# One-token decode of two attention layers and two gelu layers on one core: two K loads split into thin row groups, and three addresses and cuts moved around one V load

## The chip, the cores and the metric

The kernel runs on one core of one Trainium2 chip. The metric is the device time of one execution in microseconds (us), lower is better. Before the change three runs took 679.94, 680.22 and 680.78 us; the median is 680.22 us.

## The reference

One token (x, 512 numbers) goes through the same pair of layers twice: attention over a cache of 4096 positions with 32 heads of 128, then a gelu layer of 1376. All is float32.

```python
def _A_ref(x, k_cache, v_cache, wq, wo):
    q = (x @ wq).reshape(B, Sq, H, Dh).transpose(0, 2, 1, 3)
    scores = jnp.einsum("bhqd,bhkd->bhqk", q, k_cache) * (Dh ** -0.5)
    p = softmax(scores)
    o = jnp.einsum("bhqk,bhkd->bhqd", p, v_cache)
    return o.transpose(0, 2, 1, 3).reshape(B, Sq, H * Dh) @ wo

def _B_ref(x, w1, b1, w2, b2):
    return jnp.einsum("bsf,fd->bsd", gelu(x @ w1 + b1), w2) + b2

x = x + _A_ref(_layernorm(x), k_cache, v_cache, wq, wo)
x = x + _B_ref(_layernorm(x), w1, b1, w2, b2)
x = x + _A_ref(_layernorm(x), k_cache, v_cache, wq, wo)
x = x + _B_ref(_layernorm(x), w1, b1, w2, b2)
```

K and V are 67 MB each and are needed in both layers. SBUF does not hold them, so nearly all of both is read from HBM twice.

## The kernel before, in words

The 32 heads are worked on in G = 8 groups of J = 4. Each group has a K block and a V block of 128 partitions x 16384 numbers (8.39 MB, 64 KB a partition), and a pair of weights (a wo and a wq, 2.10 MB together). A block is cut into C = 8 chunks of 4 units; a unit (U) is 512 columns, and a chunk NC is 4 units.

All big data lies in one SBUF tile, `arena`, whose places are given by hand: three homes for blocks, A_AT, C_AT and B_AT, each 32 units long, then SHARED, SCRATCH and PAIR. Loads are made by `load` (L68 to L71): one DMA of 128 partitions, issued on SyncE's queue (SP), and kept in the order of the program. SP works through its list strictly in order: where a load must wait (for an earlier DMA, or for TensorE or another engine to be done with the place that it overwrites), every later load waits behind it. Issued transfers run on 16 DMA engines that each take their share in the order of issue.

For each group TensorE (PE) first makes the `scores` of the eight K chunks (L190), 4 matmuls a chunk. Then come the largest score, the exponentials and the sum (DVE and ACT, L195 to L218), and then `values` (L220), the product with the eight V chunks, 4 matmuls a chunk. `head_out` (L225) gathers the result (DVE writes to SCRATCH at L227 and reads it at L231) and multiplies it by wo; `next_queries` (L308) makes the next group's queries from wq. Both multiply with the pair that was loaded to PAIR, or to C_AT at the turn between the layers.

Layer one (L321 to L346) goes through groups 0 to 7; K of group g goes to RING[2g % 3] and V to RING[(2g + 1) % 3]. The generator `blocks` (L288) issues a load a piece and hands out the chunks. The last group's blocks are cut into pieces (HALVES, LAST), so that work can begin before all has landed.

At the turn, group 7's K and V and most of group 6's V are still in SBUF. So layer two goes through the groups from 7 down. Its first group (n = 0) needs no load; its second (n = 1) loads only K, in six pieces, to wherever room is, the last and longest (14 units, L374) to C_AT + 8U to C_AT + 22U. Behind it goes the pair for n = 1 (L375), to C_AT + 22U to C_AT + 30U. Six units of group 6's V were set aside in PSUM (pK) and are copied back by ACT (L384 to L387), two of them to C_AT + 30U and C_AT + 31U, where they are the values of chunk 6, j = 2 and 3. So the home C holds, while n = 1 runs: K up to unit 22, the pair up to unit 30, and two units of V.

From n = 2 on (L397) each group loads K, V and a pair again. K of n = 2 goes to A_AT and V of n = 2 to C_AT, in two pieces, five chunks and three (L403). The first needs the scores of n = 1 to be done with C's first 20 units, and the second needs the pair to be done with, which ends with `next_queries(2)` (L394).

Of the kernel before, what the change touches and what calls it, by code (L numbers as in the profile page):

```python
# [17 lines left out]
P = 128  # L18
# [5 lines left out]
C = 8  # L24
# [4 lines left out]
U = 512  # L29
NC = 4 * U  # L30
# [6 lines left out]
A_AT, B_AT, C_AT = RING  # L37
# [3 lines left out]
PAIR = SHARED + 11 * U  # L41
ARENA = PAIR + 2 * NC
HALVES = ((0, 4), (4, 8))
W1_AT_END = ((0, 2), (2, 3), (3, 4))
LAST = ((0, 4), (4, 6), (6, 7), (7, 8))
# [5 lines left out]
def decode_layers(ctx: ExitStack, tc: tile.TileContext, x, k, v, w, w1, b1, w2, b2, out):  # L51
    nc = tc.nc
# [12 lines left out]
    def at(first, n):  # L65
        return arena[:, first : first + n]

    def load(first, src):  # L68
        t = at(first, src.shape[-1])
        tc.keep_in_program_order(nc.sync.dma_start(t, src))  # L70
        return t  # L71

    def matmul(*a, **kw):
        tc.keep_in_program_order(nc.tensor.matmul(*a, **kw))  # L74

    def quarters(first):
        return [at(first + U * j, U) for j in range(4)]

    def part(src, g, a, b):
        return src[g][:, NC * a : NC * b]  # L80

    def of_w(row, i, n):
        return w[row][:, NC * i : NC * (i + n)]

    def by_four(t):
        return t.rearrange("p (j n) -> p j n", j=4)


    wq_t = by_four(load(SHARED, of_w(1, 0, 1)))
    b1c, b2c = ctile("b1c", FB), ctile("b2c", 4)  # L90
    xcol = ctile("xcol", 4)
# [62 lines left out]
    def idle(to, n=U):  # L154
        matmul(to[:, :n], zero[:, 0:1].to_broadcast([P, P]), at(C_AT, n), start=True, stop=True)
# [34 lines left out]
    def scores(z, c, kt):  # L190
        for j in range(J):
            matmul(pS[32 * j : 32 * j + C, :], z[:, j, C - 1 - c : 2 * C - 1 - c], kt[j],
                   start=(c == 0), stop=(c == C - 1))

    def exponentials(sc, nsc):  # L195
        nc.vector.tensor_reduce(ml[:, 0:1], pS, axis=AX.X, op=ALU.max)  # L196
        mt, m, bias = small("mt", 32), small("m"), small("mt", 32)
        nc.vector.transpose(mt, ml)
        nc.vector.tensor_reduce(m, mt[:, :C], axis=AX.X, op=ALU.max)
        nc.vector.tensor_scalar(mb[:, :C], m.to_broadcast([P, C]), nsc, None, op0=ALU.mult)  # L200
        nc.vector.transpose(bias, mb)  # L201
        p = at(SCRATCH, U)
        nc.scalar.activation(p, pS, AF.Exp, bias=bias[:, 0:1], scale=sc, accum_out=ml[:, 0:1])  # L203
        return p

    def weights(p):
        for b in range(4):
            tc.keep_in_program_order(nc.tensor.transpose(  # L208
                pT[:, b].rearrange("p j r -> p (j r)"), p[:, P * b : P * (b + 1)], ident))
        pt = work.tile([P, P], F32, name="turned").rearrange("p (j c b) -> p j c b", j=J, c=C)  # L210
        nc.vector.tensor_copy(pt, pT[:, :, :, :C].rearrange("p b j c -> p j c b"))  # L211
        lt, l, lr, rl = small("mt", 32), small("l"), small("mt", 32), small("rl")
        nc.vector.transpose(lt, ml)  # L213
        nc.vector.tensor_reduce(l, lt[:, :C], axis=AX.X, op=ALU.add)
        nc.vector.tensor_copy(lb, l.to_broadcast([P, 32]))
        nc.vector.transpose(lr, lb)
        nc.vector.reciprocal(rl, lr[:, 0:1])
        return pt, rl  # L218

    def values(i, pt, vt, c):  # L220
        for j in range(J):
            matmul(pO[32 * j : 32 * j + 4, :], pt[:, j, c, :], vt[j],
                   start=(i == 0), stop=(i == C - 1))

    def head_out(rl, wt, last=False):  # L225
        ot = at(SCRATCH, U)
        nc.vector.transpose(ot, pO)  # L227
        o, on = small("o", 4), on_wide
        own = at(SCRATCH, 4 * 129).rearrange("p (b q) -> p b q", q=129)[:, :, :P]
        own = own.rearrange("p b (d q) -> p d b q", q=32)[:, :, :, 0]  # L230
        nc.vector.tensor_reduce(o, own, axis=AX.X, op=ALU.add)  # L231
        if last:
            nc.vector.tensor_scalar(on[:, :4], o, rl, None, op0=ALU.mult)
        else:
            nc.vector.tensor_scalar(in_quarters(on, 4), o.unsqueeze(1).to_broadcast([P, J, 4]), rl, None,  # L235
                                    op0=ALU.mult)
        for d in range(4):
            if last:
                for j in range(J):
                    matmul(pS[32 * j : 32 * j + 1, :P], on[:, d : d + 1], wt[:, d, P * j : P * (j + 1)],  # L240
                           start=(d == 0), stop=(d == 3))
            else:
                matmul(pO, on[:, d : d + P], wt[:, d, :], start=(d == 0), stop=(d == 3))
        return of_32(turned(pS) if last else turned(pO, wide=True), 4)
# [34 lines left out]
    def load_w1(first, a, b):  # L279
        load(first + W1C * a, w1[:, W1C * a : W1C * b])  # L280

    def load_w2(first, a, b):
        load(first + U * a, w2[:, U * a : U * b])
# [1 line left out]
    def in_rows(first, n, rows):  # L285
        return [at(first + n * i, n) for i in range(rows)]

    def blocks(src, g, home, pieces=((0, C),)):  # L288
        for a, b in pieces:
            load(home + NC * a, part(src, g, a, b))  # L290
            for c in range(a, b):
                yield c, quarters(home + NC * c)

# [14 lines left out]
    def next_queries(n, xs, negm, wt):  # L308
        for c in range(4):
            matmul(pO, xs[:, 2 * c : 2 * c + P], wt[:, c, :], start=(c == 0), stop=(c == 3))  # L310
        return queries(n, negm, wide=True)

    def add_up(acc, own):
        t = small("acc", 4)
        nc.vector.scalar_tensor_tensor(t, own, 1.0, acc, op0=ALU.mult, op1=ALU.add)
        return t
# [4 lines left out]
    for g in range(G):  # L321
        final = g == G - 1
        k_home, v_home = RING[2 * g % 3], RING[(2 * g + 1) % 3]
        for c, t in blocks(k, g, k_home, HALVES if final else ((0, C),)):
            scores(z, c, t)
        pt, rl = weights(exponentials(sc, nsc))
        for c, t in blocks(v, g, v_home, LAST if final else ((0, C),)):
            values(c, pt, t, c)
            if final and c > 4:
                idle(pS)  # L330
            if g == G - 2:
                for j in range(J):
                    i = 4 * c + j - KEPT_V // U
                    if i >= 0:
                        nc.scalar.copy(pK[i], t[j])
        if final:
            wo_t = by_four(load(PAIR, of_w(g % 2, g, 1)))
            for i in range(3):
                load_w1(SHARED, i, i + 1)
            own = head_out(rl, wo_t, last=True)  # L340
            load_w1(SHARED, 3, 4)
        else:
            pair = load(PAIR, of_w(g % 2, g, 2))
            acc = add_up(acc, head_out(rl, by_four(pair[:, :NC])))
            wq_t = by_four(pair[:, NC:])
            z = next_queries(g + 1, xs, negm, wq_t)  # L346
# [8 lines left out]
    g = G - 2  # L355
# [5 lines left out]
    def begin_k(home, n):  # L361
        a = len(k_t)
        load(home, k[g][:, U * a : U * (a + n)])
        k_t.extend(at(home + U * i, U) for i in range(n))
# [4 lines left out]
    for c in range(C):  # L369
# [2 lines left out]
            begin_k(C_AT + NC * c, 4)  # L372
        if c == 5:
            begin_k(C_AT + 2 * NC, 14)  # L374
    pair = load(C_AT + 22 * U, of_w(g % 2, g - 1, 2))  # L375
    p = exponentials(sc, nsc)
    z = next_queries(1, xs, negm, wq_t)
    pt, rl = weights(p)
# [2 lines left out]
    acc = add_up(acc, head_out(rl, wo_t))  # L381

    v_t = [at(B_AT + U * i, U) for i in range(KEPT_V // U)]
    for i, first in enumerate([C_AT + 30 * U, C_AT + 31 * U] + [PAIR + U * j for j in range(4)]):  # L384
        t = at(first, U)
        nc.scalar.copy(t, pK[i])
        v_t.append(t)  # L387
# [9 lines left out]
    for n in range(2, G):  # L397
        g, final = G - 1 - n, n == G - 1
        k_home, v_home = homes[(2 * n - 1) % 3], homes[2 * n % 3]
        for c, t in blocks(k, g, k_home, HALVES if final else ((0, C),)):  # L400
            scores(z, c, t)
        pt, rl = weights(exponentials(sc, nsc))
        for c, t in blocks(v, g, v_home, LAST if final else ((0, 5), (5, 8)) if n == 2 else ((0, C),)):  # L403
            values(c, pt, t, c)
            if final and c > 4:
                idle(pS)
        if final:
            wo_t = by_four(load(PAIR, of_w(g % 2, g, 1)))
            for a, b in W1_AT_END:
                load_w1(A_AT, a, b)  # L410
            for a, b in W2_AT_END:
                load_w2(A_AT + 11 * U, a, b)
            own = head_out(rl, wo_t, last=True)
        else:
            pair = load(PAIR, of_w(g % 2, g - 1, 2))
            acc = add_up(acc, head_out(rl, by_four(pair[:, NC:])))
            z = next_queries(n + 1, xs, negm, by_four(pair[:, :NC]))
# [47 lines left out]
```

## Time and profile before

| | us |
|---|---|
| median of three runs | 680.22 |
| the profiled execution's own time | 679.55 |
| its span, first to last instruction | 677.8 |
| PE busy | 433.1 (64%) |
| weight loads | 119.4 (18%) |
| DVE busy | 110.7 (16%) |
| ACT busy | 22.2 (3%) |
| bytes moved | 286.56 MB, mean 423 GB/s |

The profile shows one execution. Times on a timeline are counted from the span's start. A row of the SP queue gives the start of an issue, what the issue itself took, the line and what is written and read; "x2" merges two issues into one row, whose length then holds the waiting between them. A line of the list of transfers gives the size and the time from the issue to the last byte's landing. A window row gives for a stretch the busy time of each engine, TensorE's granted clock, the share of time in which the DMA engines were busy, and the rate.

### The profile page before, as it was taken

To read this page: it belongs to the slowest core of one execution; us is meant where nothing else is said; L and a number is where in the kernel's file an instruction comes from. 1 tells how busy PE (TensorE), PEld (TensorE's weight loads), DVE (VectorE), ACT (ScalarE), POOL (GpSimd) and SP (SyncE) were. 2 spreads that over 40 slices of the span, in tenths; PEclk is the share of its full clock that TensorE was granted. 3 is DMA by queue.
4 is the path that set the end of the run, shared out by engine and by line. 5 is a ranking of instruction groups with operands and counts; after the bars stand their busy time and mean duration, and the time that the engine had idled before them with its cause. 6 is when DMAs were issued, how large, how long until landed. Compare 5 with 4: busy or idle time off the path is not lost. (4 is left out here: it accounts for less than half of the span.)

```text
span 677.8 us, 6359 instructions
## 1 busy us (share of the span) xinstructions
PE 433.1 (64%) x2792; PEld 119.4 (18%) x2792; DVE 110.7 (16%) x431; ACT 22.2 (3%) x47; POOL 4.3 (1%) x21
## 2 busy tenths in 40 slices
PE   1547666485554874667777897686455764766776
PEld 0112112121111211111113222221111111211112
DVE  1012101111021101210212312211021011210211
ACT  0010000000000000001000110000000000000000
POOL 1000000000000000000000000000000000000000
PEclk9969768797698876977979998998698776977977
DMA  9999999999999999999999999899999999999997
GB/s 372 434 433 433 435 433 433 416 449 437 430 433 413 451 433 430 433 431 422 428 413 359 426 459 414 358 468 441 427 433 398 465 433 423 437 430 410 426 416 294
DMA packets 11404, 286.56 MB, mean 423 GB/s; under 512 B 1776, under 2 KB 1776, under 8 KB 3440
## 3 DMA queue, kind: packets, MB, share of 16 engines
q1 hardware_dynamic: 10944, 286.14, 98.7%
q8 instruction: 22, 0.36, 0.2%
q10 hardware_dynamic: 432, 0.01, 0.0%
q14 instruction: 6, 0.05, 0.0%
HBM read 286.14 MB, written 0.00 MB: 422 GB/s over the span
## 5 line engine op out<-in xcount | busy, mean ns | idle before, releaser
L74 PE MATMUL pO<-arena,turned 128*4 128x512 f32 x1024 | 144.8, 726 | 76.8 <-DMA arena<-in_v 75.6
L74 PE MATMUL pS<-arena,zq 128*8 128x512 f32 x1024 | 137.7, 698 | 70.8 <-DMA arena<-in_k 65.4
L74 PE MATMUL pO<-arena,x_wide 128*128 128x512 f32 (+1 forms) x176 | 54.9, 508 | 24.4 <-DVE turned L137 18.1
L74 PE MATMUL pO<-arena,on_wide 128*128 128x512 f32 x112 | 51.8, 605 | 18.6 <-DVE on_wide L235 18.6
L74 PEld LDWEIGHTS pS<-arena,zq 128*8 128x8 f32 x1024 | 29.1, 99 | 176.3 <-issue 167.1
L74 PEld LDWEIGHTS pO<-arena,turned 128*4 128x4 f32 x1024 | 27.6, 97 | 183.8 <-issue 179.5
L137 DVE STREAM_TRANSPOSE turned<-pO 32x128 f32<-32x128 f32 x112 | 35.0, 312 | 101.1 <-PE pO L74 99.9
L227 DVE STREAM_TRANSPOSE arena<-pO 128x512 f32<-128x512 f32 x16 | 11.5, 717 | 220.4 <-PE pO L74 220.4
L208 PE MATMUL pO<-ident,arena 128*128 128x128 f32 x64 | 14.5, 368 | 43.9 <-ACT arena L203 42.4
L196 DVE TENSOR_REDUCE ml<-pS 128x1 f32<-128x512 f32 x16 | 11.1, 692 | 185.0 <-PE pS L74 185.0
L74 PEld LDWEIGHTS pO<-arena,x_wide 128*128 128x128 f32 (+1 forms) x176 | 21.6, 155 | 57.1 <-DVE turned L137 26.5
L203 ACT ACTIVATE arena<-pS,mt,sc 128x512 f32<-128x512 f32 x16 | 12.4, 777 | 523.7 <-DVE mt L201 523.7
L74 PEld LDWEIGHTS pO<-arena,on_wide 128*128 128x128 f32 x112 | 20.1, 189 | 51.7 <-DVE on_wide L235 31.6
L208 PEld LDWEIGHTS pO<-ident,arena 128*128 128x128 f32 x64 | 9.3, 181 | 58.6 <-ACT arena L203 51.3
L74 PE MATMUL pO<-arena,x 128*2 128x344 f32 x64 | 7.2, 531 | 5.0 <-DMA arena<-in_w 4.4
L74 PE MATMUL pS<-arena,zero 128*128 128x512 f32 x16 | 9.9, 706 | 0.0
L74 PE MATMUL pS<-arena,gelu_g 128*1 128x128 f32 x176 | 6.7, 290 | 1.5 <-DVE gelu_g L270 1.3
L213 DVE STREAM_TRANSPOSE mt<-ml 128x32 f32<-128x32 f32 x16 | 3.4, 212 | 17.2 <-ACT arena L203 17.2
L74 PEld LDWEIGHTS pS<-arena,gelu_g 128*1 128x1 f32 x176 | 3.9, 88 | 7.4 <-DVE gelu_g L270 3.7
L211 DVE COPY turned<-pO 128x128 f32<-128x128 f32 x16 | 4.4, 277 | 3.1 <-PE pO L208 3.1
L74 PE MATMUL pO<-arena,zero 128*128 128x512 f32 x8 | 4.5, 644 | 0.0
L248 POOL TENSOR_TENSOR xb<-x,b2c 128x4 f32<-128x4 f32 x2 | 0.4, 200 | 636.9 <-DVE x L148 636.9
(71 smaller groups left out, 76.5 us busy)
## 6 DMA issues: line engine op xcount, KB each, us to landing
arena<-in_w SPq DMA_DIRECT2D x13, 2048.0 KB, 28.8
arena<-in_k SPq DMA_DIRECT2D x4, 4096.0 KB, 42.5
arena<-in_v SPq DMA_DIRECT2D x2, 4096.0 KB, 47.6
arena<-in_w SPq DMA_DIRECT2D x6, 1024.0 KB, 20.3
arena<-in_v SPq DMA_DIRECT2D x1, 5120.0 KB, 23.8
arena<-in_w SPq DMA_DIRECT2D x6, 688.0 KB, 30.2
arena<-in_v SPq DMA_DIRECT2D x2, 2048.0 KB, 50.8
arena<-in_v SPq DMA_DIRECT2D x4, 1024.0 KB, 53.3
```

The lines of the kernel that those rows point to most:

```text
L74: tc.keep_in_program_order(nc.tensor.matmul(*a, **kw))
L137: nc.vector.transpose(t[q], src[q, P * j : P * (j + 1)])
L196: nc.vector.tensor_reduce(ml[:, 0:1], pS, axis=AX.X, op=ALU.max)
L203: nc.scalar.activation(p, pS, AF.Exp, bias=bias[:, 0:1], scale=sc, accum_out=ml[:, 0:1])
L208: tc.keep_in_program_order(nc.tensor.transpose(pT[:, b].rearrange("p j r -> p (j r)"), p[:, P * b : P * (b + 1)], ident))
L211: nc.vector.tensor_copy(pt, pT[:, :, :, :C].rearrange("p b j c -> p j c b"))
L213: nc.vector.transpose(lt, ml)
L227: nc.vector.transpose(ot, pO)
L248: nc.gpsimd.tensor_tensor(xb, pairs(xs)[:, :, 0], b2c, op=ALU.add)
```

## The change

It has two parts that share no line.

First, a new helper `load_uneven` issues half a K block as nine DMAs: seven of 16 rows, each of every eighth partition, and the remaining 16 rows as two of eight. It is used for the second half of K of group 1 in layer one and of n = 3 in layer two; the first half is one DMA of 128 rows.

Second, at the turn the pair for n = 1 moves up by two units, to C_AT + 24U to C_AT + 32U, and the two units of V move below it, to C_AT + 22U and 23U. V of n = 2 is cut after six chunks and no longer after five.

```diff
+    def load_uneven(first, src):
+
+        t = at(first, src.shape[-1])
+        for rows in (*(slice(k, P, 8) for k in range(7)), slice(7, 64, 8), slice(71, P, 8)):
+            tc.keep_in_program_order(nc.sync.dma_start(t[rows], src[rows]))
...
-    def blocks(src, g, home, pieces=((0, C),)):
+    def blocks(src, g, home, pieces=((0, C),), uneven=False):
         for a, b in pieces:
-            load(home + NC * a, part(src, g, a, b))
+            (load_uneven if uneven and a else load)(home + NC * a, part(src, g, a, b))
...
-        for c, t in blocks(k, g, k_home, HALVES if final else ((0, C),)):
+        for c, t in blocks(k, g, k_home, HALVES if final or g == 1 else ((0, C),), g == 1):
...
-    pair = load(C_AT + 22 * U, of_w(g % 2, g - 1, 2))
+    pair = load(C_AT + 24 * U, of_w(g % 2, g - 1, 2))
...
-    for i, first in enumerate([C_AT + 30 * U, C_AT + 31 * U] + [PAIR + U * j for j in range(4)]):
+    for i, first in enumerate([C_AT + 22 * U, C_AT + 23 * U] + [PAIR + U * j for j in range(4)]):
...
-        for c, t in blocks(k, g, k_home, HALVES if final else ((0, C),)):
+        for c, t in blocks(k, g, k_home, HALVES if final or n == 3 else ((0, C),), n == 3):
...
-        for c, t in blocks(v, g, v_home, LAST if final else ((0, 5), (5, 8)) if n == 2 else ((0, C),)):
+        for c, t in blocks(v, g, v_home, LAST if final else ((0, 6), (6, 8)) if n == 2 else ((0, C),)):
```

Only SP's list gains instructions. The first place is the start of layer one on SP, before the change: K and V of group 0, the first pair, then K and V of group 1. A name in brackets is the counter that the issue waits for: DMAHW0 to DMAHW7 are the eight counters that the DMAs use in turn, PE, DVE and Activation count the work of those engines.

```order
L70 DMA arena<-in_k 128x16384
L70 DMA arena<-in_v 128x16384 [waits DMAHW1_49,PE_49]
L70 DMA arena<-in_w 128x4096
L70 DMA arena<-in_k 128x16384
L70 DMA arena<-in_v 128x16384 [waits DMAHW4_49,DMAHW0_49,PE_49]
L70 DMA arena<-in_w 128x4096 [waits DMAHW6_49,PE_49]
```

The same place after the change, from the first pair on:

```order
L70 DMA arena<-in_w 128x4096
L70 DMA arena<-in_k 128x8192
L77 DMA arena<-in_k 16x8192 [waits DMAHW0_49,DVE_49]
L77 DMA arena<-in_k 16x8192
L77 DMA arena<-in_k 16x8192 [waits DMAHW2_49]
L77 DMA arena<-in_k 16x8192 [waits DMAHW3_49]
L77 DMA arena<-in_k 16x8192 [waits DMAHW4_49]
L77 DMA arena<-in_k 16x8192 [waits DMAHW5_49]
L77 DMA arena<-in_k 16x8192 [waits DMAHW6_49]
L77 DMA arena<-in_k 8x8192 [waits DMAHW7_49]
L77 DMA arena<-in_k 8x8192 [waits DMAHW0_49]
L70 DMA arena<-in_v 128x16384 [waits DMAHW1_49,PE_49]
```

K of group 1 waited for nothing, and V of group 1 for the scores of group 0. Now the first thin transfer waits for DVE: the count is that of the gathering read of group 0 (L231 of before). The first eight-row transfer waits for the landing of the first half (its counter is DMAHW7), the second for the landing of the first thin transfer, and V of group 1 for the landing of the second thin one. The second use, at n = 3, has the same shape, with the gathering read of n = 2.

The second place is SP's list at the turn, from the longest piece of K of n = 1 to K of n = 3. Before:

```order
L70 DMA arena<-in_k 128x7168 [waits PE_49]
L70 DMA arena<-in_w 128x4096 [waits PE_49]
L70 DMA arena<-in_k 128x16384 [waits DMAHW0_49,PE_49]
L70 DMA arena<-in_v 128x10240 [waits DMAHW5_49,DMAHW4_49,DMAHW6_49,DMAHW1_49,PE_49]
L70 DMA arena<-in_v 128x6144 [waits DMAHW2_49,DMAHW7_49,PE_49,Activation_49]
L70 DMA arena<-in_w 128x4096 [waits DMAHW3_49,Activation_49]
```

After:

```order
L70 DMA arena<-in_k 128x7168 [waits PE_49]
L70 DMA arena<-in_w 128x4096 [waits PE_49]
L70 DMA arena<-in_k 128x16384 [waits DMAHW1_49,PE_49]
L70 DMA arena<-in_v 128x12288 [waits DMAHW5_49,DMAHW6_49,DMAHW2_49,DMAHW7_49,PE_49,Activation_49]
L70 DMA arena<-in_v 128x4096 [waits DMAHW3_49,DMAHW0_49,PE_49]
L70 DMA arena<-in_w 128x4096 [waits DMAHW4_49,Activation_49]
```

The order of the loads stays. The first piece of V takes over the wait for the copied units of V (Activation), and its count of PE work moves from the scores of n = 1 to the last matmul of chunk 6 of the values of n = 1, since that matmul reads the unit at C_AT + 23U. The second piece still waits for the last matmul of `next_queries(2)`.

## Prediction

> **What bounds the kernel now.** I read the page first: the span, the busy share of the DMA engines in 40 slices, and what the queues carried.
>
> ```profile
> span 677.8 us, 6359 instructions
> DMA  9999999999999999999999999899999999999997
> GB/s 372 434 433 433 435 433 433 416 449 437 430 433 413 451 433 430 433 431 422 428 413 359 426 459 414 358 468 441 427 433 398 465 433 423 437 430 410 426 416 294
> q1 hardware_dynamic: 10944, 286.14, 98.7%
> q8 instruction: 22, 0.36, 0.2%
> ```
>
> The DMA engines are busy in nearly every slice, and queue q1, which carries the loads, fills 98.7% of their time. At 433 GB/s its 286.14 MB need 661 us of a span of 677.8 us, so only some 17 us are not plain transfer. Then I asked for the long stretches of both layers by windows.
>
> ```profile
> 70.00:340.00 270.00, 169.57 (x955) 45.23 (x956) 41.49 (x151) 9.26 (x20) 0.00 (x0) 0.81 1.00 431
> 440.00:630.00 190.00, 119.94 (x669) 32.31 (x670) 30.04 (x110) 3.56 (x9) 0.00 (x0) 0.81 1.00 433
> ```
>
> The last two columns are the DMA share and the rate: 1.00 at 431 and 433 GB/s. One of the 16 engines thus moves 433 / 16 = 27.1 GB/s. TensorE is busy for under two thirds of either stretch. Last the chain of waits, three of its pieces:
>
> ```profile
> 460.20 47.76 DMA arena<-in_k
> ...
> 547.47 47.70 DMA arena<-in_k
> ...
> 601.64 46.91 DMA arena<-in_v
> ```
>
> Where a layer runs steadily, the chain is made of transfers alone. So three things count here: bytes, pauses of the stream, and how evenly the 16 engines finish, since a block has landed when the last of them has. The bytes do not change. The sum is made against the profiled execution's own 679.55 us, 0.67 us under the median of 680.22.
>
> **The cut of V at the turn.** The slice with 358 GB/s is the turn. SP's timeline, the windows there and the list of transfers:
>
> ```profile
> 381.19 0.33 SPq L70 DMA_DIRECT2D arena<-in_w  x1
> 394.39 0.33 SPq L70 DMA_DIRECT2D arena<-in_k  x1
> 406.36 22.77 SPq L70 DMA_DIRECT2D arena<-in_v  x2
> ...
> 398.00:416.00 18.00, 14.86 (x116) 3.59 (x118) 3.95 (x16) 2.35 (x5) 0.00 (x0) 0.91 1.00 433
> ...
> 428.00:431.00 3.00, 1.36 (x10) 0.23 (x12) 1.48 (x5) 0.00 (x0) 0.00 (x0) 1.00 0.65 164
> ...
> arena<-in_k SPq DMA_DIRECT2D x1, 23.7
> ...
> arena<-in_v SPq DMA_DIRECT2D x1, 5120.0 KB, 23.8
> ...
> arena<-in_v SPq DMA_DIRECT2D x1, 3072.0 KB, 9.8
> ...
> L70 SPq DMA_DIRECT2D arena<-in_v x1: 328/328/328, 428.8 to 428.8; - x1
> ...
> 410.19 8.40 PE L74 MATMUL pO<-arena,turned 128*4 128x512 f32 x64 [0.38 <-DVE turned L211]
> ...
> 441.55 8.09 PE L74 MATMUL pO<-arena,turned 128*4 128x512 f32 x64 [0.38 <-DVE turned L211]
> ```
>
> K of n = 2 lands at 394.4 + 23.7 = 418.1 us, and five chunks of V at 406.4 + 23.8 = 430.2. The other three were issued at 428.8, when `next_queries(2)` was done with the pair, and landed 9.8 us later. Their 3.15 MB take 7.3 us at 433 GB/s, so an issue to an empty stream costs 2.5 us before it flows, and the flow began at 431.3: a pause of 1.1 us after 430.2 for the engine that was last, and of more for the others (164 GB/s from 428 to 431).
>
> After the change the first piece may go only when the values of n = 1 are through chunk 6: the 28th of 32 products, at 410.19 + 28/32 x 8.40 = 417.5 us (the row counts two matmul records a product). With 2.5 us it flows from 420.0. K has landed by 418.1, so the pause is 1.9 us, at a place where the windows show none (1.00, 433 GB/s up to 416). Its six chunks (6.29 MB, 14.5 us) then run until 434.5, and the last two, issued at 428.8 as before, follow without a pause. The pause of 1.1 us goes, one of 1.9 us comes: **+0.8 us**. If the lead-in were 2 us and not 2.5, both would shrink by the same half microsecond; only if K landed 1.9 us later against TensorE would both be hidden, so this term lies between 0 and +1. TensorE meets no V wait from it: the values of n = 2 began at 441.5 us, and 434.5 + 4.8 for the last two chunks is 439.3.
>
> Pair and copies cost nothing: the pair now waits for the last two products of the scores too, under 0.5 us, while the 3.67 MB of K ahead of it (8.5 us) are still in flight. The two units copied by ACT go to a place that is free earlier than the old one. If that cover were gone, the half microsecond would be paid.
>
> **The thin transfers: are they issued in time?** They wait for DVE's gathering read, with everything on SP behind them.
>
> ```profile
> 9.21 0.43 SPq L70 DMA_DIRECT2D arena<-in_k  x1
> 35.11 0.33 SPq L70 DMA_DIRECT2D arena<-in_v  x1
> ...
> arena<-in_k SPq DMA_DIRECT2D x1, 61.0
> ...
> 56.47 0.18 DVE L231 TENSOR_REDUCE o<-arena 128x4 f32<-128x16 f32 x1
> ...
> 450.46 0.18 DVE L231 TENSOR_REDUCE o<-arena 128x4 f32<-128x16 f32 x1
> ...
> arena<-in_k SPq DMA_DIRECT2D x1, 34.7
> ...
> 429.65 0.43 SPq L70 DMA_DIRECT2D arena<-in_k  x1
> 437.46 0.33 SPq L70 DMA_DIRECT2D arena<-in_v  x1
> ```
>
> K of group 1 landed at 9.2 + 61.0 = 70.2 us, its first half (4.19 MB, 9.7 us) thus at 60.5. The read ends at 56.65; with 2.5 us the thin transfers flow from 59.2, 1.3 us early. At n = 3 the half lands at 429.6 + 34.7 - 9.7 = 454.6 and the read ends at 450.64: 1.5 us early. Nine issues at 0.43 us are 3.9 us of SP's time; a 16-row transfer puts one row of 32 KB on each engine, 1.21 us at 27.1 GB/s, so the queue grows. V behind them was issued at 35.11 and at 437.46; now it waits for the second thin transfer's landing, at 60.5 + 2 x 1.21 = 62.9, and has to go by 70.2 - 2.5 = 67.7. All of this is covered, by about 1 us at the tightest; beyond that each microsecond of a late read would be paid. The halved K lets scores begin earlier, which gains nothing: the transfers behind them set the pace.
>
> **The thin transfers: do they flow and balance?** Seven of them give every engine a row. The two of eight rows leave it open which eight engines move them. If one is moved by one half and the other by the other, all engines carry eight rows as before, and the price is 0. If both go to the same eight, these carry nine rows and the others seven: +1.21 and -1.21 us for an engine, in each layer. The trace shows that engines do end apart:
>
> ```profile
> 670.00:672.00 2.00, 1.80 (x22) 0.60 (x24) 0.69 (x4) 0.21 (x1) 0.00 (x0) 0.50 0.96 388
> 672.00:673.00 1.00, 1.00 (x36) 0.73 (x32) 0.00 (x0) 0.00 (x0) 0.00 (x0) 0.81 0.58 234
> 673.00:674.00 1.00, 0.82 (x33) 0.49 (x28) 0.00 (x0) 0.00 (x0) 0.00 (x0) 1.00 0.40 145
> ```
>
> With nothing left behind them, about half of the engines are still at work 1 to 2 us after the first have ended. If the late ones are those relieved, up to 1.21 us a layer is gained; if any late one is among those loaded, 1.21 us is lost, since the last one counts. Which they are the trace does not say. [...] So the price lies between -1.2 and +1.2 us a layer; I take +0.4, on the side of a loss: **+0.8 us** for two. [...]
>
> Sum: +0.8 + 0.8 = +1.6 us, 681.15 for the profiled execution, 681.8 as a median. Own range of this case: from 0, below which lies the balance case of the rivals, to the upper ends, +1 and twice +1.2: 680.2 to 683.6.
>
> **The rivals.** About 0.2%, or 1.4 us, is what a measurement of this kernel can tell from no change.
>
> Thin transfers at half rate. For: no transfer of this trace has fewer than 128 rows or leaves out partitions, so the 27.1 GB/s of an engine are shown only for whole transfers; rows eight partitions apart may meet at the same few ways into SBUF while others lie idle. Against: nothing in this trace. If two engines share what one had, a row takes 2.42 us. Engines with seven rows need 16.9 us, those with nine 21.8, where 9.7 stood: +7.3 to +12.1 us in each of two layers, all on the path since the stream is the bound. With the cut of V that is +15.4 to +25.0, less up to 2 us a layer where the engines that were late are not those loaded; I would say 701. [...] The same mechanism in part (a row at 1.5 us) would give 685 to 688.
>
> Balance works (faster). The late engines of both layers are all in the relieved half: -1.2 us at each layer's end, +0.8 from V: 680.2 - 1.6 = 678.6. For: the ends lie 1 to 2 us apart, about what one row moves between the halves. Against: the engine that ends last has to be one of the relieved, and no engine of the loaded half may be over 1.2 us late, in both layers. It decides from the point where the gain of the two passes the 0.8 us of the turn.
>
> The change does nothing: the two eight-row transfers spread over both halves and the turn's two pauses weigh the same for the stream: 680.2.
>
> **How the numbers follow.** Full rate with small losses 0.43, half rate (or part of it) 0.35, balance works 0.14, nothing 0.08. Faster by over 0.2% (under 678.9): the better part of the balance case and a little of the others, 0.14. Within 0.2%: the case of nothing and the lower part of the likeliest (0 to +1.4 us), 0.24. Slower: the rest of it and the half rate, 0.62. The predicted time is that of the likeliest. The range has to reach to half rate, since 0.35 cannot be left out: from 679.2, which leaves out most of the balance case, to 704.5, which leaves out only its very end. Most of the chance lies at both ends of this range and little between 684 and 695.
>
> **What would show it.** Each thin transfer's landing tells the rate: steps of 1.2 us between successive ones at full rate, 2.4 at half. V of group 1 landing when it did before, or 7 to 12 us later, says the same. At the turn the DMA share should drop below 1 between 416 and 420 us and stay near 1 from 428 to 431 (all counted against the same event of TensorE). Balance shows at the end of the stream: fewer or more engines busy in the last 2 us. The prediction is wrong in its mechanism if the pause at the turn does not move, if the thin transfers start late, or if the stream runs slower than 27.1 GB/s an engine within them.

## The result and the profile after

The changed kernel takes 712.07 us (median of six runs, 709.71 to 714.09), the kernel before 680.50 us beside it (six runs, 679.71 to 682.26). The ratio is 1.0458, with a 95% interval of 1.0443 to 1.0474: 31 us slower, outside the range given. The profiled execution took 710.45 us, its span 708.7.

Four lines of the page of the changed kernel: the span, the busy share of the DMA engines and the rate in 40 slices, and the queue of the loads.

```profile
span 708.7 us, 6399 instructions
...
DMA  9999999999999999999999998999999999999996
GB/s 415 412 414 285 275 417 449 434 419 440 440 419 429 449 414 441 441 409 434 422 404 346 431 454 354 415 293 231 414 456 433 426 436 418 445 430 422 427 415 268
...
q1 hardware_dynamic: 11456, 286.14, 98.4%
```

The bytes are the same and the engines are as busy as before. But two pairs of slices move 285 and 275, 293 and 231 GB/s, where the kernel before moved 433 and 435, 468 and 441, and the busy share there is still 9. Each pair is a place where a half K goes in thin transfers. So the stream does not pause there; it runs slowly. Windows of the changed kernel show it in the first of the two places, with the DMA share and the rate in the last two columns:

```profile
59.00:80.00 21.00, 9.31 (x45) 2.78 (x43) 2.89 (x10) 0.00 (x0) 0.00 (x0) 0.89 1.04 206
62.00:72.00 10.00, 7.29 (x40) 2.21 (x40) 1.97 (x8) 0.00 (x0) 0.00 (x0) 1.00 1.00 211
...
86.00:200.00 114.00, 65.22 (x388) 17.04 (x380) 16.01 (x60) 2.61 (x6) 0.00 (x0) 0.81 1.00 431
```

211 GB/s at a share of 1.00 is 13.2 GB/s an engine. A row of 32 KB takes 2.48 us instead of 1.21. Behind the thin transfers the rate is 431 again, as it was.

What it costs is read where TensorE meets the loads. Its timeline before, at the values of group 1 (layer one) and of n = 3 (layer two):

```profile
89.75 9.89 PE L74 MATMUL pO<-arena,turned 128*4 128x512 f32 x64 [6.18 <-DMA arena<-in_v]
...
483.85 9.12 PE L74 MATMUL pO<-arena,turned 128*4 128x512 f32 x64 [7.40 <-DMA arena<-in_v]
```

And after, with the scores of the second half K ahead of each:

```profile
83.84 6.21 PE L80 MATMUL pS<-arena,zq 128*8 128x512 f32 x32 [12.40 <-DMA arena<-in_k]
103.10 8.55 PE L80 MATMUL pO<-arena,turned 128*4 128x512 f32 x64 [9.20 <-DMA arena<-in_v]
...
495.79 5.04 PE L80 MATMUL pS<-arena,zq 128*8 128x512 f32 x32 [17.23 <-DMA arena<-in_k]
514.74 9.23 PE L80 MATMUL pO<-arena,turned 128*4 128x512 f32 x64 [10.51 <-DMA arena<-in_v]
```

Values of group 1 begin at 103.10 instead of 89.75, 13.4 us later; those of n = 3 at 514.74 instead of 483.85, 30.9 us later. In both the bracket names the load as what ended the wait, so these are landings. Practically the whole loss stands at these two places, and none of it is won back. SP's timeline after:

```profile
57.02 8.37 SPq L77 DMA_DIRECT2D arena<-in_k  x9
67.40 0.34 SPq L70 DMA_DIRECT2D arena<-in_v  x1
```

The nine thin transfers are issued from 57.0 us on, and V behind them at 67.4, long before the thin ones have landed. Issue was not the trouble.

### The profile page after: what moved, and what is told of

Its sections match the earlier page's. It is cut to its first block, busy times and chain, and to the rows that moved or that the text cites. A ratio compares the mean times of both kernels' runs of the same rounds, so it can differ in the third digit from the quotient of the medians.

```text
span 708.7 us, 6399 instructions
## 1 busy us (share of the span) xinstructions
PE 433.9 (61%) x2792; PEld 119.5 (17%) x2792; DVE 110.4 (16%) x431; ACT 22.2 (3%) x47; POOL 4.3 (1%) x21
## 5 line engine op out<-in xcount | busy, mean ns | idle before, releaser
L80 PE MATMUL pO<-arena,turned 128*4 128x512 f32 x1024 | 146.7, 734 | 85.0 <-DMA arena<-in_v 83.7
L80 PEld LDWEIGHTS pO<-arena,on_wide 128*128 128x128 f32 x112 | 20.1, 189 | 51.7 <-DVE on_wide L241 31.6
## 6 DMA issues: line engine op xcount, KB each, us to landing
arena<-in_w SPq DMA_DIRECT2D x6, 688.0 KB, 30.1
```

## The experiments

What had to be told apart: ways into SBUF, as I supposed them, that the rows under way share (theory 1), a fixed time for each transfer that is not overlapped (theory 2), and the reading side, where 16 streams 512 KB apart might collide (theory 3). Then the size of the other terms: the cut of V, and the nine and seven rows. Costs in us are the ratio less 1, times 680.5, with the 95% interval. Rates are taken from the window 62 to 72 us, which lies within the thin transfers; only in the two kernels that flow at nearly the full rate does its end belong to the V behind them. The share of a short window can pass 1, so the rate is divided by it. A transfer of 16 rows is 524 KB. The diffs show the lines that matter, and "..." stands for what is left out.

**The two parts alone.** Only the cut of V, with the pair and the two copied units:

```diff
-    pair = load(C_AT + 22 * U, of_w(g % 2, g - 1, 2))
+    pair = load(C_AT + 24 * U, of_w(g % 2, g - 1, 2))
...
-    for i, first in enumerate([C_AT + 30 * U, C_AT + 31 * U] + [PAIR + U * j for j in range(4)]):
+    for i, first in enumerate([C_AT + 22 * U, C_AT + 23 * U] + [PAIR + U * j for j in range(4)]):
...
-        for c, t in blocks(v, g, v_home, LAST if final else ((0, 5), (5, 8)) if n == 2 else ((0, C),)):
+        for c, t in blocks(v, g, v_home, LAST if final else ((0, 6), (6, 8)) if n == 2 else ((0, C),)):
```

> Only the move of the pair behind chunk six of C and the cut of the third V into six and two chunks; K loads as before. If the thin transfers carry nearly all of the 31.6 us that the change cost, this kernel is slower than before by 0.8 us (my term, 0 to +1) to 1.4 us (what the landings of V behind the turn gained on those of K in the changed kernel: +15.9 against +14.5 us), so 681.3 to 681.9. If the cut had a cost that shows only later (a pair or copy that comes late), it is slower by over 2 us.

Measured 681.42, ratio 1.0013 (1.0001 to 1.0025): +0.9 us (0.1 to 1.7). Windows at the turn, of the kernel before and then of this one; 428 to 431 before was 0.65 and 164 GB/s:

```profile
416.00:420.00 4.00, 2.67 (x29) 0.47 (x17) 1.13 (x3) 0.00 (x0) 0.00 (x0) 1.00 0.88 379
...
412.00:442.00 30.00, 22.53 (x148) 6.49 (x140) 6.65 (x24) 0.87 (x2) 0.00 (x0) 0.96 0.91 382
```

```profile
416.00:420.00 4.00, 2.67 (x25) 0.54 (x18) 1.13 (x3) 0.00 (x0) 0.00 (x0) 1.00 0.66 197
428.00:431.00 3.00, 1.35 (x10) 0.23 (x12) 1.48 (x5) 0.00 (x0) 0.00 (x0) 1.00 1.13 481
...
412.00:442.00 30.00, 22.53 (x148) 6.67 (x144) 6.65 (x24) 0.87 (x2) 0.00 (x0) 0.96 0.89 371
```

The pause has moved from 428 to 431 to 416 to 420. Over the 30 us around both it costs (382 - 371) x 30 us = 0.33 MB, or 0.8 us at 433 GB/s.

Only the thin transfers:

```diff
-        for c, t in blocks(k, g, k_home, HALVES if final else ((0, C),)):
+        for c, t in blocks(k, g, k_home, HALVES if final or g == 1 else ((0, C),), g == 1):
...
-        for c, t in blocks(k, g, k_home, HALVES if final else ((0, C),)):
+        for c, t in blocks(k, g, k_home, HALVES if final or n == 3 else ((0, C),), n == 3):
```

> Only the thin K transfers of both layers; the cut of V as before. If the two edits add up, 31.6 less 0.8 to 1.4: slower than before by 30 to 31 us, 710.5 to 711.5, some 15 us per layer. If the cut of V pushed the second use into a worse place, the thin transfers alone cost less than 28 us.

Measured 706.94, ratio 1.0383 (1.0364 to 1.0403): +26.1 us (24.8 to 27.4), below what was expected. The two parts make 27.0 us, the whole 31.2 (30.1 to 32.3).

**What makes the rows slow?** The same half K in eight transfers of columns, all 128 rows each (this kernel and the others of this part change the same lines and leave the cut of V as before):

```diff
-        for rows in (*(slice(k, P, 8) for k in range(7)), slice(7, 64, 8), slice(71, P, 8)):
-            ...dma_start(t[rows], src[rows])
+        for k in range(8):
+            cut = slice(n * k, n * k + n)
+            ...dma_start(t[:, cut], src[:, cut])
```

> The same two half Ks in eight transfers of 512 KB, each 1,024 columns of all 128 rows, so that one engine still gets eight pieces and the issue count stays about the same. If the half rate comes from which rows are under way together (rows eight apart share only half of the ways into SBUF), these run at the full 27 GB/s per engine: 680.2 to 682 in all, a step of 1.2 us between landings. If it comes from cutting a load into many small transfers (a fixed price for each, some 1.2 us per transfer in the changed kernel's steps of 2.5 us), the cost stays: 8 x 1.2 = 9.7 us per layer, about 699.

Measured 683.97, ratio 1.0042 (1.0027 to 1.0057): +2.9 us. Its window:

```profile
62.00:72.00 10.00, 8.26 (x52) 2.65 (x56) 1.62 (x6) 0.00 (x0) 0.00 (x0) 1.00 1.17 478
```

478 / 1.17 = 409 GB/s: eight transfers of the same 524 KB flow at nearly the full rate, so a fixed time for each is out. Pieces of 4 KB run at 409 and not at 431 GB/s, which for 8.4 MB makes 1.0 us; the rest of the 2.9 was not followed up.

Nine transfers of every fourth row of one half of the partitions, the two halves in turn. The first has only eight rows, so that eight engines are to be a row ahead of the others (a lead) and work on the other half:

```diff
+        for rows in (slice(3, 32, 4), slice(64, P, 4), slice(0, 64, 4), slice(65, P, 4), slice(1, 64, 4),
+                     slice(66, P, 4), slice(2, 64, 4), slice(67, P, 4), slice(35, 64, 4)):
```

> The same nine transfers (two of eight rows and seven of 16), the same bytes per transfer and the same nine and seven rows per engine, but of every fourth row: rows 0 to 60 or 64 to 124 (offset by up to three), so that the rows under way together are four apart over half of the partitions. If the rows eight apart were limited by shared ways into SBUF, and the engines' two halves now stand in different groups of rows most of the time, the rate is full or well above half: steps of 1.2 to 1.6 us, 679 to 690 in all, and the part that is left is the price of the nine and seven rows. If thin transfers of one row per engine are slow whatever the rows are, the steps stay at 2.4 to 2.5 us and the time at 708 to 712.

Measured 697.14, ratio 1.0240 (1.0216 to 1.0263): +16.3 us, between the two. The first window lies in layer one, the second in layer two:

```profile
62.00:72.00 10.00, 6.37 (x39) 1.72 (x37) 1.48 (x5) 0.00 (x0) 0.00 (x0) 1.00 0.96 224
466.00:475.00 9.00, 5.12 (x36) 1.16 (x34) 1.48 (x5) 0.00 (x0) 0.00 (x0) 1.00 1.14 295
```

224 / 0.96 = 233 and 295 / 1.14 = 259 GB/s: better than the changed kernel's 211, far from full. Neither theory had said this.

So the rows themselves were moved. Sixteen neighbouring rows:

```diff
+        for k in range(8):
+            rows = slice(16 * k, 16 * k + 16)
```

> The two half Ks in eight transfers of 16 neighbouring rows (0 to 15, 16 to 31 and so on) instead of every eighth row; still one row per engine and transfer, no nine and seven. [...] The reading side (16 streams 512 KB apart in the source collide): the streams are now 64 KB apart as neighbours, so full rate, about 680 to 684. A fixed time per transfer that the next transfer on the same engine does not overlap (about 1.0 to 1.3 us when an engine has only one row of it): steps of 2.2 to 2.5 us as before, +8 to +10 per layer, 696 to 701.

Measured 734.25, ratio 1.0781 (1.0690 to 1.0872): +53 us.

```profile
62.00:72.00 10.00, 7.14 (x40) 2.04 (x40) 1.48 (x5) 0.00 (x0) 0.00 (x0) 1.00 1.16 138
```

138 / 1.16 = 119 GB/s, 4.4 us a row: a little over a quarter. Theory 3 had 680 to 684 us here and theory 2 696 to 701; only theory 1 leaves room for less than half the rate. To part writing from reading, near rows read and far ones written, and the reverse:

```diff
+            near, far = slice(16 * k, 16 * k + 16), slice(k, P, 8)
+            ...dma_start(t[far], src[near])
```

> Each transfer reads 16 neighbouring rows and writes them to every eighth row of the tile, so K's rows stand in another order and the output is another; only its time counts. Ways into SBUF: the writes are those of the changed kernel, half the rate, about 700. Reading side: full rate, 680 to 684. Fixed time per transfer: 696 to 701.

```diff
+            ...dma_start(t[near], src[far])
```

> The reverse: each transfer reads every eighth row and writes 16 neighbouring rows; K's rows again stand in another order. [...] Reading side: as the changed kernel's thin transfers, half the rate, about 700. Fixed time per transfer: 696 to 701.

Measured 706.51, ratio 1.0374 (1.0270 to 1.0477), and 732.59, ratio 1.0757 (1.0694 to 1.0819). The window of the first, then of the second:

```profile
62.00:72.00 10.00, 6.11 (x38) 1.54 (x36) 1.48 (x5) 0.00 (x0) 0.00 (x0) 1.00 0.99 207
```

```profile
62.00:72.00 10.00, 6.68 (x40) 1.81 (x38) 1.48 (x5) 0.00 (x0) 0.00 (x0) 1.00 1.19 144
```

207 / 0.99 = 209 and 144 / 1.19 = 121 GB/s. (The first time lies 6 us above the 700 that theory 1 gave; the second is within 2 us of the 734.25 of rows that were neighbours on both sides.) The rate follows the rows that are written; where they are read from changes next to nothing (211 and 209 GB/s into every eighth row, 119 and 121 into 16 neighbouring ones). Theory 3 is out. Next, two rows per engine in a transfer, every fourth of all 128:

```diff
+        for k in range(4):
+            rows = slice(k, P, 4)
```

> The two half Ks in four transfers of every fourth row (32 rows of 32 KB, two per engine). Fixed time per transfer of 1.0 to 1.3 us: four of them per layer, so steps of 3.4 to 3.7 us and +4 to +5 us per layer, 689 to 691. Ways into SBUF or the reading side with half the rate for every row: steps of 4.8 us, +9.7 per layer, about 700. Full rate, were the two rows of an engine enough to spread it: 680 to 683.

Measured 682.33, ratio 1.0029 (1.0010 to 1.0048): +2.0 us.

```profile
62.00:72.00 10.00, 8.36 (x52) 2.45 (x56) 1.48 (x5) 0.00 (x0) 0.00 (x0) 1.00 1.07 460
```

460 / 1.07 = 430 GB/s. I had expected half the rate here, since I thought that the first rows of all engines meet as in the thin transfers. They don't. That left two readings: either the reach of a transfer's rows counts (how widely they spread over the partitions), or one row per engine is what is slow. Two more kernels tell these apart, with four and with two rows per engine but neighbouring ones:

```diff
+        for rows in (slice(0, 64), slice(64, P)):
```

> Each half K in two transfers of 64 neighbouring rows (four rows of 32 KB per engine): rows 0 to 63, then 64 to 127. [...] If only one row per engine is slow, full rate: 680 to 683.

```diff
+        for rows in [slice(32 * k, 32 * k + 32) for k in range(4)]:
```

> Each half K in four transfers of 32 neighbouring rows (two per engine). [...] If closeness as such counts (32 neighbouring rows between 16 at 4.35 us and 128 at 1.21), slower than two transfers of 64. If only one row per engine is slow: 680 to 683.

Measured 705.78, ratio 1.0374 (1.0322 to 1.0426), and 705.31, ratio 1.0367 (1.0325 to 1.0409). Again the window of the first and of the second:

```profile
62.00:72.00 10.00, 6.53 (x39) 1.72 (x37) 1.48 (x5) 0.00 (x0) 0.00 (x0) 1.00 1.00 207
```

```profile
62.00:72.00 10.00, 7.29 (x40) 2.21 (x40) 1.72 (x7) 0.00 (x0) 0.00 (x0) 1.00 1.01 211
```

207 and 209 GB/s. So one row per engine is not what is slow: which rows a transfer writes counts, and 64 neighbouring rows go no faster than 32. (At these rates a half K of 4.19 MB takes 20.1 to 20.3 us instead of 9.7, which for two makes about 701; both times are some 4 us above it, and the measurement does not say why.) Last, every fourth row of one half without the eight engines' lead:

```diff
+        for rows in [slice(a + k, a + 64, 4) for k in range(4) for a in (64, 0)]:
```

> As the nine transfers of every fourth row of one half, in turn from the upper and the lower half, but eight transfers of 16 rows, so no eight engines are a row ahead and every engine has eight rows. If the lead had parted the engines onto different halves part of the time, steps go from 2.0 to 2.2 us up to 2.4: 700 to 702, more than the 697 with nine rows. If the lead did nothing and only the ninth row goes, 2.0 to 2.2 us by eight rows: 692 to 697.

Measured 700.26, ratio 1.0293 (1.0261 to 1.0324).

```profile
62.00:72.00 10.00, 6.92 (x40) 1.92 (x38) 1.48 (x5) 0.00 (x0) 0.00 (x0) 1.00 0.95 211
466.00:475.00 9.00, 5.97 (x26) 1.89 (x28) 2.89 (x10) 0.00 (x0) 0.00 (x0) 1.00 1.00 226
```

211 / 0.95 = 222 and 226 GB/s, half the rate; with the lead it was 233 and 259. That the lead parted the engines somewhat is my reading; no run shows which rows an engine writes.

**The nine and seven rows.** The thin transfers alone, but the last 16 rows as one transfer:

```diff
+        for rows in [slice(k, P, 8) for k in range(8)]:
```

> As the thin transfers alone (V cut as before), but the eighth is every eighth row too, 16 rows, so every engine has eight rows. If the whole cost is the rate of the slow rows and the engine with most rows ends last, nine rows of 2.53 us cost 13.1 us per layer over eight of 1.21, eight rows 10.5: 5 us less than the thin transfers alone in all, 702. If nine and seven cost nothing beside the rate, 706 to 707 as there.

Measured 702.26, ratio 1.0325 (1.0296 to 1.0354): +22.1 us (20.1 to 24.1). TensorE's timeline of this kernel, and then of the thin transfers alone:

```profile
81.89 5.97 PE L80 MATMUL pS<-arena,zq 128*8 128x512 f32 x32 [11.87 <-DMA arena<-in_k]
101.02 8.37 PE L80 MATMUL pO<-arena,turned 128*4 128x512 f32 x64 [9.31 <-DMA arena<-in_v]
...
506.87 8.54 PE L80 MATMUL pO<-arena,turned 128*4 128x512 f32 x64 [8.63 <-DMA arena<-in_v]
```

```profile
83.50 5.64 PE L80 MATMUL pS<-arena,zq 128*8 128x512 f32 x32 [13.08 <-DMA arena<-in_k]
102.67 9.72 PE L80 MATMUL pO<-arena,turned 128*4 128x512 f32 x64 [10.13 <-DMA arena<-in_v]
...
510.37 8.97 PE L80 MATMUL pO<-arena,turned 128*4 128x512 f32 x64 [8.33 <-DMA arena<-in_v]
```

The ninth row makes K land 1.6 us later (83.50 - 81.89) and V 1.65, and by n = 3 it is 3.5 us. The same unevenness with three quarters of the rows in transfers of 32 rows at the full rate; the last 32 go as eight, 16 and eight rows of one half:

```diff
+        for rows in (slice(0, P, 4), slice(1, P, 4), slice(2, P, 4),
+                     slice(3, 32, 4), slice(67, P, 4), slice(35, 64, 4)):
```

> Nine rows for eight engines and seven for the other eight, at nearly the full rate: three transfers of every fourth row (32 rows, two per engine), then the 32 rows left as eight, 16 and eight. V cut as before. If an engine's share of the bytes is what makes it late, the engines with seven rows gain 1.2 us per layer on the others and the layers end up to 1.2 us earlier: 679.5 to 681. [...]

Measured 687.52, ratio 1.0094 (1.0070 to 1.0119): +6.4 us, 4.4 more than four transfers of 32 rows. Its window:

```profile
62.00:72.00 10.00, 7.16 (x40) 2.06 (x40) 1.48 (x5) 0.00 (x0) 0.00 (x0) 1.00 1.11 417
```

417 / 1.11 = 376 GB/s, where the four transfers had 430. So this kernel does not hold the full rate. As an estimate, the last 32 rows (1.05 MB) at the 222 GB/s that fourths of one half showed in the kernel without the lead take 4.7 us instead of 2.4: 4.6 us for two uses, as much as the whole excess. The slow rows and the unevenness are not parted here, and no gain from a relieved engine shows. TensorE's timeline of the four transfers, and then of this kernel:

```profile
91.20 8.77 PE L81 MATMUL pO<-arena,turned 128*4 128x512 f32 x64 [13.48 <-DMA arena<-in_v]
...
485.91 9.38 PE L81 MATMUL pO<-arena,turned 128*4 128x512 f32 x64 [11.15 <-DMA arena<-in_v]
```

```profile
91.54 8.70 PE L80 MATMUL pO<-arena,turned 128*4 128x512 f32 x64 [11.93 <-DMA arena<-in_v]
...
488.77 9.75 PE L80 MATMUL pO<-arena,turned 128*4 128x512 f32 x64 [10.29 <-DMA arena<-in_v]
```

The estimate has 2.3 us at each use. In these two executions V is 0.3 us later at the first use and 2.9 at the second, so they confirm its sum better than its parts.

**Do the parts hurt each other?** The whole change with four transfers of every fourth row, and the changed kernel once more:

```diff
-        for rows in (*(slice(k, P, 8) for k in range(7)), slice(7, 64, 8), slice(71, P, 8)):
+        for rows in [slice(k, P, 4) for k in range(4)]:
```

> The whole change, its cut of V too, but each half K in four transfers of every fourth row. If the slow rows are the whole of the thin transfers' cost, the parts add up: before + 0.9 (cut of V) + 1.5 (four transfers) = 683.3, between 682 and 684.5. If the two edits hurt each other whatever the rate (together they cost 31.6 us, one by one 27.0), 686 to 688.

> The changed kernel once more, on the same chip as the other three, to see whether the 4.6 us by which it exceeds its two parts are there again (711 to 713) or came from the chip (706 to 708).

Measured 682.77, ratio 1.0032 (1.0019 to 1.0045), +2.2 us, where the parts by themselves make 0.9 and 2.0: there they add up. The changed kernel took 709.46, ratio 1.0431 (1.0395 to 1.0468), +29.3 us (26.9 to 31.8). That overlaps both the 27.0 of the parts and the 31.2 of the first time (the parts ran on another chip than this repetition), so an excess of some 2 to 4 us is not well measured, and no cause of it is shown. In the profiled executions it is not at the first place: there the changed kernel is 0.4 us behind the thin transfers alone (103.10 against 102.67), but 4.4 behind at n = 3 (514.74 against 510.37), of which the cut of V is 0.9. In the repetition these are 0.8 and 2.0. No kernel of these beat the one before.

## Why the prediction was wrong

**What bounds the kernel** held. The stream is the bound, and each microsecond lost in it shows at the end: 30.9 us at n = 3, 31 us in the time.

**The cut of V** held: +0.8 us said, +0.9 measured, with the pause moved to where it was placed. Pair and copies cost nothing that shows.

**Issued in time** held: the first thin transfer was issued at 57.0 us and the DMA share stayed at 1.04 through 59 to 80 us.

**The thin transfers' flow** is the step that failed. The sum put one row of 32 KB at 1.21 us, from the 27.1 GB/s that an engine has in transfers of all 128 rows, and gave that 0.43; with the two rivals that rest on the same rate, the balance that works and the change that does nothing, it had 0.65. It was 2.48 us, 13.2 GB/s an engine, which is one of the signs of being wrong that the prediction named. The rival of half rate had 2.42 us, at 0.35, and had noted that the full rate was shown for whole transfers only. That should have counted for more: a row of the trace is a price for what it shows, and here the rows to be moved were of another kind. By the rows that are written, the windows give 431 GB/s for all 128 and 430 for every fourth of 128; 209 to 211 for every eighth, 209 for 32 neighbouring, 207 for 64 neighbouring and 222 to 226 for every fourth of one half (233 and 259 with the lead); 119 and 121 for 16 neighbouring. These rates show that the rows written together share a limit. The ways into SBUF are my picture of it; no run shows them.

**The price within that rival**, 701, was too low as well. It took the middle of seven rows (+7.3 a layer) and nine (+12.1), less a part for engines that were late and would not be loaded. But the engines with nine rows end last, so nine rows count: 9 x 2.48 - 9.7 = +12.6 us a layer, two of them and the cut of V +26.1, or 706.6. The thin transfers alone measured 706.94, and without the cut of V they should by this be 705.7. A row at 2.48 and not 2.42 us is the lesser part. With eight rows it is 8 x 2.48 - 9.7 = +10.1 a layer, 700.8; measured 702.26. What the whole change costs beyond its parts is not explained.

**The balance.** I took +0.4 us a layer between -1.2 and +1.2, and for a gain in both layers 0.14. No run shows this term at the full rate: the one arrangement tried cost 4.4 us more than eight rows for every engine, but by the estimate above its slow last rows can account for that by themselves. At half rate the ninth row counts in full: 4.7 us for two uses (706.94 against 702.26). So both eight-row transfers went to the same eight engines, as I read it: were they spread, K would not land 1.6 us later (83.50 against 81.89) than with eight equal rows. Which eight it was no run shows, nor whether the relief of the others can bring a gain at the full rate.

**The chances** put 0.62 on slower, which it was, but the predicted time was that of a case that did not occur, and the range ended 7.6 us short.

## What to carry to other kernels

Cut a load by columns, or by rows that still reach over all partitions (every fourth row of 128 at two rows an engine ran at 430 GB/s), where a load has to be cut; here the two cost 2.9 and 2.0 us and won nothing. A block of 64 rows or every eighth row halved the stream here (207 and 211 GB/s, against 431) while the engines looked fully busy (a share of 1.00). When a DMA share of 1 goes with a low rate, look at which partitions are written, not at issue or bytes. And take a rate from the trace only for transfers of the shape that the trace holds: where the shape is new, its rate is the first unknown, and deserves the most chance.

## What the runs showed of the hardware that I had not expected

A share of 1.00 can mean 433, 211 or 119 GB/s (1.16 and 138 in the window of 16 neighbouring rows). So the share counts an engine as busy while its rows move at a half or a quarter of the rate.

Every fourth row of all 128 partitions in one transfer ran at the full rate (430 GB/s), although 16 rows of every eighth ran at half (211). Why the 32 rows do not slow each other stays open; no run here shows which engine wrote which row.
